# Filled waits, a gate spread by DMA and closer attention in a one-core attention and expert kernel

## The chip, the cores and the metric

The kernel runs on one core of a Trainium2 chip. A core has TensorE (PE) for matrix products into the accumulator memory (PSUM), VectorE (DVE), ScalarE (ACT) and GpSimd (POOL) for the rest, SyncE (SP) for issuing transfers, and 16 DMA engines. The metric is the device time of one execution in microseconds (us); before the change it is 210.46 us, the median of three runs (210.33 to 211.22).

## What is computed

Eight sequences of 576 positions and eight heads of 64 pass through a linear attention (softmax of q over the head's width, softmax of k over the positions), and then each whole sequence goes to one of eight experts, chosen from the mean of the attention's output:

```python
q_s = softmax(q, axis=-1)                       # [8, 8, 576, 64]
k_s = softmax(k, axis=2)
kv  = einsum('bhsd,bhse->bhde', k_s, v)
x   = einsum('bhsd,bhde->bhse', q_s, kv)        # then [8, 576, 512]
logits = x.mean(axis=1) @ w_gate                # [8, 8]
e = argmax(logits, axis=1); gate = softmax(logits)[e]
out[b] = gate[b] * (relu(x[b] @ w1[e[b]]) @ w2[e[b]])   # w1 [512, 1024], w2 [1024, 512]
```

For the inputs drawn here the experts are 2, 3, 3, 1, 3, 3, 4, 6, so five of the eight sequences need an expert that is not yet in the core's memory.

## The kernel before

A sequence has two units n = 2b and 2b + 1 of four heads each. For a unit q, k and v are loaded by SyncE (576 KB each), ScalarE takes the exponentials, VectorE sums q, GpSimd casts v and scales q, TensorE makes the products "kv" and the transposes of q, and then two products x. A gate follows the second unit: it picks the expert, and GpSimd issues the loads of w1 and w2, which are cast to 16 bits on the way. The expert of sequence b takes 17 steps; the work of later sequences is put between the steps by a table of ticks, where one expert spans 17 ticks. [...] The first two sequences' attention runs ahead of the table (the prologue). Cuts are marked; `in_pool` has three buffers each for q, k and v, the pool of output tiles has four, and the PSUM banks are: "mm" three, "kv" two, "ht" one, "x" one of double width.

```python
    def load(n, names="qkv"):
        if n >= 2 * B:
            return
        b, i = divmod(n, 2)
        for name in names:
            x = in_pool.tile([128, 2, J * Dh], FP32, name=f"{name}_in")
            nc.sync.dma_start(out=x, in_=pair_src({"q": q, "k": k, "v": v}[name], b, i))
            ins[n, name] = x.rearrange("p n (j d) -> p n j d", j=J)
    # ... cut ...
    def kv_mm(n):
        ek, va, kps = halves[n]["ek"], v_aug[n % NVB], kv_banks(n)
        for j in range(J):
            for g in range(2):
                r = slice(64 * g, 64 * g + 64)
                nc.tensor.matmul(
                    kps[g][:, 0:129], lhsT=ek[r, j], rhs=va[r, j],
                    start=(j == 0), stop=(j == J - 1),
                )
    # ... cut ...
    def t_mm(n):
        eq, kps = halves[n]["eq"], t_banks(n)
        for j in range(J):
            for g in range(2):
                r = slice(64 * g, 64 * g + 64)
                tp = kps[g].bitcast(FP16)[:, 448:448 + S]
                nc.tensor.transpose(out=tp[:, 64 * j:64 * j + 64], in_=eq[r, j], identity=ident[r, r])
    def t_out(n, g):
        tp = t_banks(n)[g].bitcast(FP16)[:, 448:448 + S]
        qt = qt_pool.tile([128, S], FP16, name="qt")
        if n < 4 or (n < 8 and g == 1):
            nc.scalar.copy(qt, tp)
        else:
            nc.vector.tensor_copy(out=qt, in_=tp)
        halves[n]["qt"][g] = qt
    # ... cut ...
    # x_step(n, g), sequence b = n // 2, c = 2 * (n % 2) + g
        kvs, qts = halves[n]["kv"], halves[n]["qt"]
        px = bank("x")
        nc.tensor.matmul(px[:, 0:SM], lhsT=kvs[g], rhs=qts[g][:, 0:SM], start=True, stop=True)
        nc.tensor.matmul(px[:, SM:S], lhsT=kvs[g], rhs=qts[g][:, SM:S], start=True, stop=True)
        if b < 2:
            if c == 0 or n == 3:
                nc.vector.tensor_copy(out=xt[:, c, :], in_=px[:, 0:S])
            else:
                nc.scalar.copy(xt[:, c, :], px[:, 0:S])
        else:
            nc.vector.tensor_tensor_reduce(
                out=xt[:, c, :], in0=px[:, 0:S], in1=ones_f32.to_broadcast([128, S]),
                scale=1.0, scalar=0.0, op0=ALU.mult, op1=ALU.add, accum_out=pooled[:, c:c + 1],
            )
    # ... cut ...
    # q_sum_step(n): sums of scaled q, a bank 'mm' and a bank 'ht' for a sequence
        qbar = seqs[b]["qbar"]
        for g in range(2):
            c = 2 * i + g
            r = slice(64 * g, 64 * g + 64)
            qb = seqs[b]["qb"][g][:, 4 * i:4 * i + 4]
            for j in range(J):
                nc.tensor.matmul(
                    qb, lhsT=eq[r, j], rhs=qhl[r, j].rearrange("p h n -> p (h n)"), start=(j == 0), stop=(j == J - 1)
                )
    # ... cut ...
    def gate_step(b):
        pooled = seqs[b]["pooled"]
        pg = kv_banks(2 * b + 1)[0][:, 136:144] if b > 1 else seqs[b]["qb"][0][:, 64:96]
        for c in range(ND):
            nc.tensor.matmul(
                pg[0:1, 0:E], lhsT=pooled[:, c:c + 1], rhs=wg_sb[:, c, :],
                start=(c == 0), stop=(c == ND - 1),
            )
        mx8 = gat_pool.tile([1, 8], FP32, name="mx8")
        nc.vector.max(out=mx8, in_=pg[0:1, 0:E])
        eidx = gat_pool.tile([1, 8], U32, name="eidx")
        nc.vector.max_index(out=eidx, in_max=mx8, in_values=pg[0:1, 0:E])
        # ... history of experts, slot, whether the expert is fresh (small VectorE steps) ...
        nc.vector.tensor_copy(out=hist[:, slot:slot + 1], in_=eidx[0:1, 0:1])
        zz = gat_pool.tile([1, E], FP32, name="zz")
        nc.vector.tensor_copy(out=zz, in_=pg[0:1, 0:E])
        # ... expert number into a GpSimd register, then two or four DMAs of w1 ...
    # ... cut ...
    def warm(count):
        pw = bank("ht")
        for n in range(count):
            nc.tensor.matmul(pw[:, 0:128], lhsT=ident, rhs=blkmask, start=True, stop=True)
    def hold_loads(b):
        nc.sync.dma_start(out=held, in_=w1_all[64:65, b, ND - 1, F - 8:F])
    def gate_exp(b):
        ex = gat_pool.tile([1, E], FP32, name="ex")
        sm = gat_pool.tile([1, 1], FP32, name="sm")
        nc.scalar.activation(out=ex, in_=seqs[b]["zz"], func=AF.Exp, bias=seqs[b]["nmx"], scale=1.0 / S, accum_out=sm)
        seqs[b]["sm"] = sm
    # ... cut ...
    def gate_spread(b):
        pb = bank("x")
        nc.tensor.matmul(pb[:, 0:2], lhsT=ones_row, rhs=seqs[b]["hl"], start=True, stop=True)
        gate = gat_pool.tile([128, 1], FP32, name="gate")
        nc.vector.tensor_single_scalar(out=gate, in_=pb[:, 1:2], scalar=1.0 / 2048.0, op=ALU.mult)
        nc.vector.tensor_tensor(out=gate, in0=gate, in1=pb[:, 0:1], op=ALU.add)
        seqs[b]["gate"] = gate
    # ... cut ...
    # fetch(b, w_all, part): VectorE copies the expert from the slot that holds it (onto itself if fresh)
    # moe(b): the expert on one sequence, 17 steps: 8 groups, 4 blocks in two halves, a tail
            phm = bank("mm")
            fsl = slice(fc * 128, (fc + 1) * 128)
            for c in range(ND):
                nc.tensor.matmul(
                    phm, lhsT=w1_sb[:, c, fsl], rhs=xt[:, c, 0:SM],
                    start=(c == 0), stop=(c == ND - 1),
                )
            for c in range(ND):
                nc.tensor.matmul(
                    pht[:, fc * ST:(fc + 1) * ST], lhsT=w1_sb[:, c, fsl], rhs=xt[:, c, SM:S],
                    start=(fc == 0 and c == 0), stop=(fc == NF - 1 and c == ND - 1),
                )
        ...
        gate = seqs[b]["gate"]
        for st in range(4):
            po = bank("mm")
            for fc in range(NF):
                nc.tensor.matmul(
                    po, lhsT=hsb[:, fc, st * 128:st * 128 + 128], rhs=w2_sb[:, fc, :],
                    start=(fc == 0), stop=(fc == NF - 1),
                )
                if fc == 3:
                    yield
            osb = o_pool.tile([128, D], FP32, name="osb")
            nc.scalar.mul(osb, po, gate)
            for jj in range(2):
                nc.sync.dma_start(out=out_p[b, :, 2 * st + jj], in_=osb[64 * jj:64 * jj + 64])
            yield
    # ... cut ...
    # the table: at(t, function, arguments)
    # at_gate(t, b): gate_step at t, gate_exp t + 3, gate_split t + 4, gate_spread t + 6
    at(0, pool_step, 1)
    at(1, t_step, 2)
    at_gate(0.2, 1)
    at(0.4, hold_loads, 1)
    at(0.4, load, 4)
    at(0.4, load, 5)
    at(0.4, load, 6)
    at(0.3, mul_q, 2, nc.vector)
    at(2.5, mul_q, 3, nc.vector)
    at(2, x_step, 2, 0)
    at(3, x_step, 2, 1)
    at(4.5, t_step, 3)
    at(6, x_step, 3, 0)
    at(7, x_step, 3, 1)
    at(13, load_w2, 1)
    at(5, gate_exp, 0)
    at(5.5, gate_split, 0)
    at(6.5, gate_spread, 0)
    places = [(19.5, 24), (29.5, 34), (39.5, 44.5), (56, 61), (73, 78), (90, 95)]
    for b in range(2, B):
        for i in range(2):
            n, t = 2 * b + i, places[b - 2][i]
            at(t, kvt_step, n)
            for g in range(2):
                at(t + 2 + 2 * g, x_step, n, g)
            at(t - 5.35, exp_q, n)
            at(t - (5.35 if n < 8 else 8), cast_v, n)
            at(t - 4.35, exp_k, n)
            if n + 3 < 2 * B:
                at(t - 4.35, load, n + 3)
            at(t - 4.7, scale_q, n, nc.gpsimd)
        at_gate(places[b - 2][1] + 5, b)
    # ... cut ...
    with tc.manual_schedule(engines={ET.PE, ET.DVE, ET.Activation, ET.Pool, ET.SP}):

        warm(55)
        # ... attention of the first two sequences, unit by unit ...
        q_sum_step(3)
        kv_step(3)
        for b in range(B):
            for m, _ in enumerate(moe(b)):
                run_ticks(NU * b + m + 1)
```

## Time and profile before

| | before |
|---|---|
| time, median of 3 | 210.46 us |
| span of the profiled execution | 209.2 us |
| first product of the first expert | 26.7 us |
| second expert's first product | 52.4 us |
| TensorE's last product | 204.1 us |
| bytes moved by DMA | 48.56 MB |

The page of a profile gives each engine's busy time and share of the span, then the span in 40 slices of 5.2 us, in which a digit is a busy share in tenths; PEclk is the clock granted to TensorE in tenths of full speed. Waits are listed as "engine line <- what released it: total us, times, longest". The chain of waits follows the work that ended last back through what released each piece. A line such as L435 is a line of the kernel's file: L181 is the products "kv", L202 the transposes, L241 the products x, L294 the gate's product, L401 the product that spreads the gate, L435 and L440 the expert's first layer, L454 and L469 its second, L418 the copy of an expert, L119 a load, L463 and L476 the stores, L380 the held load. SPq, POOLq and ACTq are the issuing queues. In the list of groups, the costliest on GpSimd, VectorE and ScalarE are these:

```profile
L444 ACT ACTIVATE hsb<-mm 128x512 f16<-128x512 f32 x64 | 37.5, 593 | 26.6 <-PE mm L435 26.0
L461 ACT ACTIVATE osb<-mm,gate 128x512 f32<-128x512 f32 x32 | 21.9, 687 | 40.1 <-PE mm L454 33.1
L154 POOL TENSOR_TENSOR eq<-eq,qsi 128x1152 f16<-128x1152 f16 x13 | 27.5, 2119 | 36.2 <-DVE qsi L143 19.8
...
L141 DVE TENSOR_REDUCE qs<-eq 128x18 f32<-128x1152 f16 x16 | 21.5, 1346 | 16.1 <-ACT eq L124 16.1
```

Behind the count stand the busy time in us and the mean of one in ns, then the idle time of the engine just before, and what ended most of it.

### The profile page before, as it was taken

The numbers are of one execution on the slowest core, as the hardware profiler recorded it, in microseconds if no ns is written. First come the engines' busy times: TensorE is split into PE (matmuls) and PEld (weight loads), VectorE is DVE, ScalarE is ACT, GpSimd is POOL, SyncE is SP. The second block draws the span as 40 slices with busy tenths as digits, with TensorE's granted clock in tenths as the row PEclk, the third lists the DMA queues.
The fourth block names the chain that finished last, engine by engine and source line by source line (L and its number), as shares of the span: only waits on it lengthen the run. The fifth ranks groups of instructions, "written<-read, shape, count | busy, mean of one in ns | idle before, by whom it ended". The sixth has DMA issues, their size and how long they took to land.

```text
span 209.2 us, 4699 instructions
## 1 busy us (share of the span) xinstructions
PE 176.8 (85%) x1743; PEld 96.1 (46%) x1743; DVE 112.7 (54%) x378; ACT 112.8 (54%) x178; POOL 62.2 (30%) x71
## 2 busy tenths in 40 slices
PE   6455798979979489488999679998999899999990
PEld 6443544434535146244455334564555455445440
DVE  0667853461484767538665476766669663222000
ACT  2686514836766535745349613892398146536630
POOL 2163905000760650232905151156047405000000
PEclk9955555999999969979999999999999999999998
DMA  6999999999989999776999994592469947996054
GB/s 181 380 391 392 130 183 191 182 231 387 395 318 301 403 393 382 265 238 140 185 293 273 372 395 106 115 326 64 98 106 188 214 119 136 194 190 200 0 128 99
DMA packets 28583, 48.56 MB, mean 232 GB/s; under 512 B 2960, under 2 KB 10128, under 8 KB 28560
## 3 DMA queue, kind: packets, MB, share of 16 engines
q1 hardware_dynamic: 19472, 37.76, 54.0%
q0 software_dynamic: 8544, 10.49, 31.8%
q8 instruction: 13, 0.21, 0.4%
q10 hardware_dynamic: 544, 0.02, 0.2%
q14 instruction: 10, 0.08, 0.1%
HBM read 61.88 MB, written 9.44 MB: 341 GB/s over the span
## 4 chain that ended last, share of the span: by engine, by line
PE 45%; DMA 25%; DVE 21%; issue 4%; ACT 2%; SPq 1%; POOL 0%; POOLq 0%; DVEq 0%; ACTq 0%
PE mm L454 17%; PE mm L435 14%; DMA w_all<-in_moe_w_dram 12%; DMA q_in<-in_q_dram 7%; DVE qs L141 6%; DMA v_in<-in_v_dram 6%; PE kv L181 4%; PE mm L469 3%; DVE w_all L418 2%; PE x L241 2%; DVE kv L191 2%; PE ht L440 2%; DVE qt L210 2%; ACT eq L124 2%; DVE qsi L143 1%
## 5 line engine op out<-in xcount | busy, mean ns | idle before, releaser
L435 PE MATMUL mm<-xt,w_all 128*128 128x512 f16 x256 | 69.2, 402 | 1.4 <-ACT hsb L444 1.4
L454 PE MATMUL mm<-w_all,hsb 128*128 128x512 f16 x256 | 61.9, 387 | 0.1
L444 ACT ACTIVATE hsb<-mm 128x512 f16<-128x512 f32 x64 | 37.5, 593 | 26.6 <-PE mm L435 26.0
L461 ACT ACTIVATE osb<-mm,gate 128x512 f32<-128x512 f32 x32 | 21.9, 687 | 40.1 <-PE mm L454 33.1
L154 POOL TENSOR_TENSOR eq<-eq,qsi 128x1152 f16<-128x1152 f16 x13 | 27.5, 2119 | 36.2 <-DVE qsi L143 19.8
L454 PEld LDWEIGHTS <-hsb 128*128 128x128 f16 x256 | 23.3, 99 | 27.3 <-issue 2.1
L435 PEld LDWEIGHTS <-w_all 128*128 128x128 f16 x256 | 21.2, 101 | 21.3 <-issue 6.0
L141 DVE TENSOR_REDUCE qs<-eq 128x18 f32<-128x1152 f16 x16 | 21.5, 1346 | 16.1 <-ACT eq L124 16.1
L418 DVE COPY w_all<-w_all 128x2048 f16 x28 | 21.6, 773 | 15.1 <-DMA w_all<-in_moe_w_dram 14.4
L132 POOL CAST va<-v_in 128x1152 f16<-128x1152 f32 x15 | 18.5, 1233 | 32.0 <-PE mm L469 17.4
L250 DVE CUSTOM_DVE_ANT_0 xt<-x,ones_f 128x576 f16<-128x576 f32 x24 | 17.8, 743 | 14.6 <-PE x L242 14.6
L440 PEld LDWEIGHTS <-w_all 128*128 128x128 f16 x256 | 17.0, 101 | 17.0 <-issue 3.3
L241 PE MATMUL x<-qt,kv 128*128 128x512 f16 x32 | 13.4, 419 | 10.2 <-DVE pooled L250 4.5
L346 POOL DMA_DIRECT2D w_all<-in_moe_w_dram x18 | 8.0, 448 | 46.0 <-DVE nmx L328 22.9
L124 ACT ACTIVATE eq<-q_in 128x1152 f16<-128x1152 f32 x16 | 18.5, 1159 | 2.1 <-DMA q_in<-in_q_dram 2.1
L136 ACT ACTIVATE ek<-k_in 128x1152 f16<-128x1152 f32 x16 | 18.6, 1164 | 0.5 <-DMA k_in<-in_k_dram 0.5
L440 PE MATMUL ht<-xt,w_all 128*128 128x64 f16 x256 | 18.6, 197 | 0.0
L181 PE MATMUL kv<-va,ek 64*128 64x129 f16 x288 | 13.8, 241 | 3.4 <-DVE zz L323 3.3
L208 ACT COPY qt<-kv 128x576 f16<-128x576 f16 x10 | 6.1, 638 | 14.6 <-DVE kv L191 11.6
L181 PEld LDWEIGHTS <-ek 64*128 64x128 f16 x288 | 10.2, 105 | 6.9 <-issue 6.2
L191 DVE SCALAR_TENSOR_TENSOR kv<-kv,icv,blkmask 128x128 f16<-128x128 f32 x32 | 11.2, 351 | 1.2
L189 DVE RECIPROCAL icv<-kv 128x1 f32<-128x1 f32 x32 | 5.1, 158 | 8.7 <-PE kv L202 7.2
(80 smaller groups left out, 141.0 us busy)
## 6 DMA issues: line engine op xcount, KB each, us to landing
w_all<-in_moe_w_dram POOLq DMA_DIRECT2D x30, 512.0 KB
q_in<-in_q_dram SPq DMA_DIRECT2D x16, 576.0 KB, 6.5
k_in<-in_k_dram SPq DMA_DIRECT2D x16, 576.0 KB, 7.6
v_in<-in_v_dram SPq DMA_DIRECT2D x16, 576.0 KB, 8.8
out_dram<-osb SPq DMA_DIRECT2D x64, 128.0 KB, 4.3
w_all<-in_moe_w_dram POOLq DMA_DIRECT2D x4, 256.0 KB
out_dram<-osb_t SPq DMA_DIRECT2D x16, 64.0 KB, 2.4
wg_sb<-in_moe_w_gate_dram ACTq DMA_DIRECT2D x2, 8.0 KB, 5.3
```

What stands on the lines that cost most here:

```text
L124: nc.scalar.activation(out=eq.rearrange("p j n d -> p n j d"), in_=ins.pop((n, "q")), func=AF.Exp)
L132: nc.gpsimd.tensor_copy(out=dst, in_=ins.pop((n, "v")))
L136: nc.scalar.activation(out=ek.rearrange("p j n d -> p n j d"), in_=ins.pop((n, "k")), func=AF.Exp)
L141: nc.vector.tensor_reduce(out=qs, in_=halves[n]["eq"], op=ALU.add, axis=AX.X)
L154: eng.tensor_tensor(out=eq, in0=eq, in1=qsi.unsqueeze(3).to_broadcast([128, J, 2, Dh]), op=ALU.mult,)
L181: nc.tensor.matmul(kps[g][:, 0:129], lhsT=ek[r, j], rhs=va[r, j], start=(j == 0), stop=(j == J - 1),)
L418: copy = nc.vector.tensor_copy(out=w_all[:, b % NS, cs, fs], in_=w_all[:, ds(seqs[b]["src"], 1), cs, fs].rearrange("p o c f -> p (o c) f"),)
L435: nc.tensor.matmul(phm, lhsT=w1_sb[:, c, fsl], rhs=xt[:, c, 0:SM], start=(c == 0), stop=(c == ND - 1),)
L440: nc.tensor.matmul(pht[:, fc * ST:(fc + 1) * ST], lhsT=w1_sb[:, c, fsl], rhs=xt[:, c, SM:S], start=(fc == 0 and c == 0), stop=(fc == NF - ...
L444: nc.scalar.activation(out=hsb[:, fc, 0:SM], in_=phm, func=AF.Relu)
L454: nc.tensor.matmul(po, lhsT=hsb[:, fc, st * 128:st * 128 + 128], rhs=w2_sb[:, fc, :], start=(fc == 0), stop=(fc == NF - 1),)
L461: nc.scalar.mul(osb, po, gate)
```

## The change

Four things change together. Idle products ("warm") are put ahead of products that wait in the prologue, with counts set by the table FILL, and the opening run grows from 55 to 80; their results are not used, they keep TensorE active. The gate's value is spread over the 128 partitions by a small DMA from ScalarE's queue, where before it went as two halves through a product and two VectorE steps; and the gate's product moves from a "kv" bank to the "x" bank, with its copy taken earlier. The attention of the third and fourth sequences (units 4 to 7) moves closer together in the table, with one of each unit's two x results taken out of PSUM by ScalarE and the transposed q all by VectorE. Loads from unit 7 on are issued later and further apart. The numbers of the units' ticks are in `places`.

```diff
@@ -108,6 +108,9 @@
 
     out_p = out.rearrange("b (p j) d -> b p j d", j=J)
 
+
+    FILL = {("qsum", 0): 0, ("t", 0): 24, ("qsum", 1): 18, ("x", 0, 0): 8, ("qsum", 2): 30, ("qsum", 3): 14}
+
     ins, halves, seqs, issued, copies = {}, {}, {}, {}, {}
 
     def load(n, names="qkv"):
@@ -195,6 +198,7 @@
 
     def t_mm(n):
         eq, kps = halves[n]["eq"], t_banks(n)
+        warm(FILL.get(("t", n), 0), kps[0][:, 144:208])
         for j in range(J):
             for g in range(2):
                 r = slice(64 * g, 64 * g + 64)
@@ -204,7 +208,7 @@
     def t_out(n, g):
         tp = t_banks(n)[g].bitcast(FP16)[:, 448:448 + S]
         qt = qt_pool.tile([128, S], FP16, name="qt")
-        if n < 4 or (n < 8 and g == 1):
+        if n < 4:
             nc.scalar.copy(qt, tp)
         else:
             nc.vector.tensor_copy(out=qt, in_=tp)
@@ -238,6 +242,7 @@
         xt, pooled = seqs[b]["xt"], seqs[b].get("pooled")
         kvs, qts = halves[n]["kv"], halves[n]["qt"]
         px = bank("x")
+        warm(FILL.get(("x", c, b), 0), px[:, 640:768])
         nc.tensor.matmul(px[:, 0:SM], lhsT=kvs[g], rhs=qts[g][:, 0:SM], start=True, stop=True)
         nc.tensor.matmul(px[:, SM:S], lhsT=kvs[g], rhs=qts[g][:, SM:S], start=True, stop=True)
         if b < 2:
@@ -246,6 +251,8 @@
                 nc.vector.tensor_copy(out=xt[:, c, :], in_=px[:, 0:S])
             else:
                 nc.scalar.copy(xt[:, c, :], px[:, 0:S])
+        elif n < 8 and g:
+            nc.scalar.activation(out=xt[:, c, :], in_=px[:, 0:S], func=AF.Copy, accum_out=pooled[:, c:c + 1])
         else:
             nc.vector.tensor_tensor_reduce(
                 out=xt[:, c, :], in0=px[:, 0:S], in1=ones_f32.to_broadcast([128, S]),
@@ -261,6 +268,7 @@
             seqs.setdefault(b, {})["qb"] = [bank("mm"), bank("ht")]
             seqs[b]["qbar"] = gat_pool.tile([128, ND, 2, 4], FP16, name="qbar")
         qbar = seqs[b]["qbar"]
+        warm(FILL["qsum", n], seqs[b]["qb"][1][:, 256:384])
         for g in range(2):
             c = 2 * i + g
             r = slice(64 * g, 64 * g + 64)
@@ -288,8 +296,7 @@
 
     def gate_step(b):
         pooled = seqs[b]["pooled"]
-
-        pg = kv_banks(2 * b + 1)[0][:, 136:144] if b > 1 else seqs[b]["qb"][0][:, 64:96]
+        pg = bank("x") if b > 1 else seqs[b]["qb"][0][:, 64:96]
         for c in range(ND):
             nc.tensor.matmul(
                 pg[0:1, 0:E], lhsT=pooled[:, c:c + 1], rhs=wg_sb[:, c, :],
@@ -300,6 +307,8 @@
         nc.vector.max(out=mx8, in_=pg[0:1, 0:E])
         eidx = gat_pool.tile([1, 8], U32, name="eidx")
         nc.vector.max_index(out=eidx, in_max=mx8, in_values=pg[0:1, 0:E])
+        zz = gat_pool.tile([1, E], FP32, name="zz")
+        nc.vector.tensor_copy(out=zz, in_=pg[0:1, 0:E])
         slot = b % NS
         sidx = None
         if b:
@@ -319,8 +328,6 @@
             sidx = gat_pool.tile([1, 8], U32, name="sidx")
             nc.vector.max_index(out=sidx, in_max=top, in_values=score)
         nc.vector.tensor_copy(out=hist[:, slot:slot + 1], in_=eidx[0:1, 0:1])
-        zz = gat_pool.tile([1, E], FP32, name="zz")
-        nc.vector.tensor_copy(out=zz, in_=pg[0:1, 0:E])
 
         gone = (b + 2) % NS
         nc.vector.memset(hist[:, gone:gone + 1], -1.0)
@@ -369,11 +376,13 @@
             )
         part_loads(b)
 
-    def warm(count):
-
-        pw = bank("ht")
+    def warm(count, pw=None):
+
+        if pw is None:
+            pw = bank("ht")[:, 0:128]
+        width = pw.shape[1]
         for n in range(count):
-            nc.tensor.matmul(pw[:, 0:128], lhsT=ident, rhs=blkmask, start=True, stop=True)
+            nc.tensor.matmul(pw, lhsT=ident, rhs=blkmask[:, 0:width], start=True, stop=True)
 
     def hold_loads(b):
 
@@ -385,23 +394,15 @@
         nc.scalar.activation(out=ex, in_=seqs[b]["zz"], func=AF.Exp, bias=seqs[b]["nmx"], scale=1.0 / S, accum_out=sm)
         seqs[b]["sm"] = sm
 
-    def gate_split(b):
+    def gate_value(b):
         gt = gat_pool.tile([1, 1], FP32, name="gt")
         nc.vector.reciprocal(out=gt, in_=seqs[b]["sm"])
-        hl = gat_pool.tile([1, 2], FP16, name="hl")
-        nc.vector.tensor_copy(out=hl[:, 0:1], in_=gt)
-        nc.vector.tensor_scalar(
-            out=hl[:, 1:2], in0=hl[:, 0:1], scalar1=gt, scalar2=-2048.0, op0=ALU.subtract, op1=ALU.mult
-        )
-        seqs[b]["hl"] = hl
+        seqs[b]["gt"] = gt
 
     def gate_spread(b):
 
-        pb = bank("x")
-        nc.tensor.matmul(pb[:, 0:2], lhsT=ones_row, rhs=seqs[b]["hl"], start=True, stop=True)
         gate = gat_pool.tile([128, 1], FP32, name="gate")
-        nc.vector.tensor_single_scalar(out=gate, in_=pb[:, 1:2], scalar=1.0 / 2048.0, op=ALU.mult)
-        nc.vector.tensor_tensor(out=gate, in0=gate, in1=pb[:, 0:1], op=ALU.add)
+        nc.scalar.dma_start(out=gate, in_=seqs[b]["gt"].to_broadcast([1, 128]))
         seqs[b]["gate"] = gate
 
     def fetch(b, w_all, part):
@@ -491,8 +492,8 @@
     def at_gate(t, b):
         at(t, gate_step, b)
         at(t + 3, gate_exp, b)
-        at(t + 4, gate_split, b)
-        at(t + 6, gate_spread, b)
+        at(t + 4.5, gate_value, b)
+        at(t + 6.5, gate_spread, b)
 
     at(0, pool_step, 1)
     at(1, t_step, 2)
@@ -509,23 +510,23 @@
     at(6, x_step, 3, 0)
     at(7, x_step, 3, 1)
     at(13, load_w2, 1)
-    at(5, gate_exp, 0)
-    at(5.5, gate_split, 0)
-    at(6.5, gate_spread, 0)
-    places = [(19.5, 24), (29.5, 34), (39.5, 44.5), (56, 61), (73, 78), (90, 95)]
+    at(1.5, gate_exp, 0)
+    at(2.7, gate_value, 0)
+    at(4.7, gate_spread, 0)
+    places = [(20, 23.5), (27, 31), (40, 45), (56, 61), (73, 78), (90, 95)]
     for b in range(2, B):
         for i in range(2):
             n, t = 2 * b + i, places[b - 2][i]
             at(t, kvt_step, n)
             for g in range(2):
-                at(t + 2 + 2 * g, x_step, n, g)
+                at(t + 2 + g * (1.5 if n < 8 else 2), x_step, n, g)
             at(t - 5.35, exp_q, n)
             at(t - (5.35 if n < 8 else 8), cast_v, n)
             at(t - 4.35, exp_k, n)
-            if n + 3 < 2 * B:
-                at(t - 4.35, load, n + 3)
             at(t - 4.7, scale_q, n, nc.gpsimd)
-        at_gate(places[b - 2][1] + 5, b)
+            if n >= 7:
+                at(max(places[(n - 3) // 2 - 2][(n - 3) % 2] - 4.3, t - 15), load, n)
+        at_gate(places[b - 2][1] + (4.7 if b < 4 else 5), b)
         at(places[b - 2][1] + 9, load_w2, b)
     for b in range(1, B):
         for part in range(2):
@@ -549,7 +550,7 @@
     load(2)
     with tc.manual_schedule(engines={ET.PE, ET.DVE, ET.Activation, ET.Pool, ET.SP}):
 
-        warm(55)
+        warm(80)
         exp_q(0)
         sum_q(0)
         q_sum_step(0)

```

## The prediction

> **What bounds the kernel now.** I read the page first (busy shares, the row of slices), then TensorE's waits, then the chain of waits in order of time, then the timelines of TensorE and of the load queue, and asked in each stage which wait ends last.
>
> The page:
>
> ```profile
> PE 176.8 (85%) x1743; PEld 96.1 (46%) x1743; DVE 112.7 (54%) x378; ACT 112.8 (54%) x178; POOL 62.2 (30%) x71
> ...
> PEclk9955555999999969979999999999999999999998
> DMA  6999999999989999776999994592469947996054
> ```
>
> TensorE is the busiest engine, but 32 us of the 209.2 us span it is idle, and in slices 3 to 7 (about 10 to 37 us) it runs at half clock. The DMA engines are busy almost without a break in the first 125 us. So there are two bounds: transfers in the first half, TensorE in the second.
>
> TensorE's waits by stage, 0 to 70, 70 to 130 and 130 to 210 us:
>
> ```profile
> PE mm L269 <- DVE qhl L149: 4.9, 4, 2.3
> PE kv L202 <- DVE eq L154: 2.7, 2, 1.8
> PE mm L435 <- ACT hsb L444: 1.4, 1, 1.4
> ```
>
> ```profile
> PE kv L181 <- DVE zz L323: 3.3, 2, 1.9
> PE x L241 <- DVE pooled L250: 3.0, 2, 1.8
> PE x L241 <- DVE gate L404: 3.0, 1, 3.0
> PE x L241 <- DVE qt L210: 1.7, 1, 1.7
> ```
>
> ```profile
> PE x L241 <- DVE pooled L250: 1.5, 2, 0.9
> ```
>
> The columns are the total in us, times, and the longest. The 11.0 us of the middle stage are the target: 3.3 because a gate shares the "kv" bank with the next sequence's products, 3.0 because the gate's spreading matmul takes TensorE and the "x" bank. From 131.7 us on only 1.5 us are lost.
>
> The chain, in order of time (start, us):
>
> ```profile
> 32.82 9.04 DMA w_all<-in_moe_w_dram
> ...
> 42.76 6.56 DMA q_in<-in_q_dram
> 49.38 12.39 DMA v_in<-in_v_dram
> ...
> 102.35 15.40 DMA w_all<-in_moe_w_dram
> ```
>
> The third sequence's loads (units 4 and 5) may start only when the second sequence's first weights have landed (41.9 us, the held load), and then queue: unit 4's q lands at 49.3, its v at about 52.4, unit 5's v at 56.9, unit 6's v at 61.8 us. The last line is the fourth sequence's w2: issued from 101.6, landed at 117.85 us, and the in-order VectorE stood before it from 113.2 us.
>
> TensorE's timeline where the third and fourth sequences enter:
>
> ```profile
> 55.45 0.70 PE L181 MATMUL kv<-va,ek 64*128 64x129 f16 x18
> 55.99 0.43 PE L202 MATMUL kv<-ident,eq 64*128 64x64 f16 x18
> ...
> 63.68 0.70 PE L181 MATMUL kv<-va,ek 64*128 64x129 f16 x18
> ```
>
> ```profile
> 73.83 0.69 PE L181 MATMUL kv<-va,ek 64*128 64x129 f16 x17 [1.89 <-DVE zz L323]
> ...
> 81.67 0.70 PE L181 MATMUL kv<-va,ek 64*128 64x129 f16 x18
> ```
>
> These are units 4, 5, 6, 7. Units 4 and 5 come 3 and 7 us after their last input; unit 6 comes 12 us after its v, by its place in the program, not by a transfer.
>
> **What the skill says.** The Trainium skill, "TensorE: Matmul & The Clock Gate", Part 1, says the clock is halved by default, full after some 3.4 us of sustained activity and halved again after an idle window of that length. The trace agrees on the way up: after 33.2 us, with no gap, the clock was full at about 37.2. On the way down it is stricter: waits of 1.0 and 1.8 us (7.3 to 8.3 and 8.9 to 10.7) were enough, the clock was 0.50 from 10 us. So I count gaps of about 3 us, or two near each other, as a fall. The same page's Part 4 says that transposes don't count as activity in the same way; nothing here separates that. "DMA: Bandwidth & Descriptors", Anatomy of one DMA, gives a fixed cost of about 2 us; the smallest output stores here take 2.4 us at the median. It thus costs more latency than the matmul it replaces, but on no compute engine. Its specifications put the memory limit per core at about 358 GB/s; the trace moves 380 to 403 GB/s, and the trace decides.
>
> **The change part by part.**
>
> (1) Fill. The 55 warm-up matmuls took 5.41 us, 98 ns on average. The same page's Part 1 gives 107 ns for this width cold and 56 ns warm, which fits a mix; as an estimate, 25 more at 56 ns end at 7.30 + 1.4 = 8.7 us, 0.4 us after their successor is ready (8.26). The 24, 18, 8, 30 and 14 fills take by the same figure at most 1.3, 1.0, 0.45, 1.7 and 0.8 us, in waits of 1.83, 1.32, 0.73, 2.32 and 0.26 us; only the last overruns, by up to 0.5 us. If the clock stays full, the first four groups of the first expert cost 1.0 instead of 2.0 us, about 4 us, with transposes and x products 4.5. They cannot start earlier, since the first weights land at 26.7 us. Against this, the transposes of unit 2 wait longer for VectorE's multiply (about 2.0 instead of 0.84 us).
>
> (2) Spreading the gate by DMA removes the two waits of 1.03 and 0.44 us at 42 us. By (1) and (2) the first expert ends at about 47.1 instead of 52.4 us: 26.75 + 8 groups of 0.98 + transposes and x products 1.6 + gate 0.4 + waits 2.6 = 39.2, then 6.9 and 1.0 us.
>
> (3) Most of that is given back at unit 4. Its values land at 52.4 us whatever TensorE does; GpSimd needs 1.16 us for the cast and 2.12 us for the multiply, so its transposes start at 55.7 us, as before (55.99). TensorE arrives there at about 51 us with four groups done instead of three, so 1.0 us is kept, and the wait can cost up to 2 us of cold clock. I count 0 for parts (1) to (3) together.
>
> (4) Closer attention. From 56.3 us on: unit 5 needs v at 56.9 + 1.16 + 2.12 = 60.2 and runs at 60.7 to 61.7 (before to 64.6, one group further): gain 1.9 us. Unit 6 is ready at 61.8 + 1.16 + 2.12 = 65.1, and TensorE is there at 65.8. Unit 7's loads now stand behind all ten stores of the first sequence; I expect q at 67 and v at 70, ready at about 71.7, TensorE there at 71.0. The second expert ends at about 74 us; VectorE has some 19 us of work in these 18 us, so I add 2 us: 76 instead of 80.75 us, with unit 7 already done, which before came after. Gain so far 4.75 + 1.4 (one unit: 0.64 + 0.31 + two x of 0.22).
>
> (5) The third expert with units 8 and 9: 15.9 + 2 x 1.4 + gate 0.3 + 1.0 = 20 us, so the fourth starts at 96 instead of 108.7 us. What goes is the 2.98 and 1.39 us of waits and their cold clock (88.3 to 92 us, 1.5 us), with unit 7's work.
>
> (6) The fourth expert's weights. Its gate comes after the second group of the third expert, at about 78.5 us instead of 94.7. Weights then fly from 80 us; they share with units 10 and 11 and the stores, 22 us before, so w2 lands at about 101, needed by VectorE at 100 and TensorE at 104. So the stall at 118 to 123 us (1.75 + 1.23) goes: 20 us for the fourth expert with units 10 and 11, and the fifth starts at 116 instead of 131.7 us.
>
> (7) From there the order is nearly unchanged: 77.5 us, less some tenths for the spreading matmul. Sum: 116 + 77.5 = 193.5 us of span; the measured time was 1.26 us above the span (210.46 to 209.2), so 194.8, and 195 with a little for the cold wait of (3).
>
> **Rivals.** (a) Transfers become the bound throughout. By the fourth expert's second half they must have carried 12 units (21.2 MB), three experts (12.6 MB as read; 4.2 each, since weights are read as 32 bits) and three sequences' stores (3.5 MB): 37.3 MB at 390 GB/s is 96 us, with the start and the gap at 20 to 22 us about 101, against my 104. There is little slack; if queue order wastes 5 us, the time is 199 to 201. The load queue speaks for it: its stores waited 5.5 us on v loads. (b) VectorE, 19 us of work in 18 us of the dense stage, or ScalarE held by its own small DMA issues, becomes the bound: 2 to 4 us more, 197 to 199. (c) The fills delay real work and the early wait at unit 4 keeps the clock low: nothing is gained before 60 us and 2 us are lost, 197. (d) Nothing is gained, since the same stalls return elsewhere: 208 to 211. Against it speaks that 6.3 us of the middle waits come from banks that are no longer shared in that way.
>
> **Range and chances.** All rivals but (d) stay under 203 us. If the dense stage fits without the 2 us of (4) and the cold clock does not return, 191. I say 195 us, 190 to 203 in 8 of 10. Faster by over 2% needs under 206.3: 0.93; within 2%: 0.05; slower: 0.02.
>
> **What would show it.** A clock of 1.0 from 10 to 40 us and the first expert's second half from about 39 us show (1) and (2). A wait of TensorE of 3 to 5 us ahead of unit 4's products, which stay at 54 to 57 us, shows (3); if they come before 53, (3) is wrong and the time lower. Units 6 and 7 at about 66 and 71.5 us show (4). Weights of the fourth expert in flight at 80 to 101 us, and no VectorE wait for them, show (6); a wait there is rival (a). The waits on the gate's spread and on its copy from the "kv" bank should be gone.

## The result and the profile after

The changed kernel takes 201.04 us, the median of four runs (200.41 to 202.59); four runs of the kernel before on the same chip took 210.41 us (210.33 to 211.22). The ratio is 0.956, with a 95% interval of 0.950 to 0.962. That is 9.4 us gained, of 15.5 that the prediction promised. The profiled run is the slowest of the four (202.59 us, a span of 200.9), so its moments lie up to 2 us later than those of a typical run. Its mean granted clock is also the lowest, 0.964 against 0.978 to 0.979 in the other three. The reader should keep that in mind wherever a single moment is read.

The page of the changed kernel: busy times, and two rows of the span in 40 slices of 5.0 us.

```profile
PE 176.4 (88%) x1854; PEld 98.1 (49%) x1854; DVE 114.0 (57%) x342; ACT 112.8 (56%) x182; POOL 61.9 (31%) x71
...
PEclk9999965899999969999999999999999999999999
DMA  5999999999996997988999959794999966995054
```

TensorE does the same work (176.4 us) in a span that is 8.3 us shorter. The clock row, half speed in slices 3 to 7 before, is full up to 25 us; then it falls after all, in slices 6 and 7 (25 to 35 us), just when the first expert begins, and once more in slice 15 (70 to 75 us). In the other three executions, whose mean clock is higher, the loss was probably smaller; they have no trace.

TensorE's waits of the changed kernel, at 0 to 70 us and at 70 to 125 us (total in us, times, longest):

```profile
PE mm L277 <- DVE qhl L152: 2.5, 3, 1.2
...
PE x L246 <- DVE pooled L257: 1.8, 1, 1.8
PE kv L206 <- DVE eq L157: 1.8, 2, 1.0
```

```profile
PE x L301 <- ACT xt L255: 3.0, 1, 3.0
PE x L246 <- DVE pooled L257: 1.9, 2, 1.6
```

The two causes that the change aimed at are gone: no wait on the gate's spread, none on its copy out of the "kv" bank. In their place stands a new one of 3.0 us, the gate's product (L301), which now takes an "x" bank and gets it only when ScalarE has taken the last x product out. TensorE's timeline shows where:

```profile
54.12 0.70 PE L184 MATMUL kv<-va,ek 64*128 64x129 f16 x18
...
60.21 0.38 PE L246 MATMUL x<-qt,kv 128*128 128x512 f16 x1 [1.84 <-DVE pooled L257]
60.55 0.70 PE L184 MATMUL kv<-va,ek 64*128 64x129 f16 x18
...
65.61 0.70 PE L184 MATMUL kv<-va,ek 64*128 64x129 f16 x18
70.51 0.35 PE L301 MATMUL x<-wg_sb,pooled 128*1 128x8 f32 x8 [2.96 <-ACT xt L255]
...
76.09 0.38 PE L246 MATMUL x<-qt,kv 128*128 128x512 f16 x1 [1.62 <-DVE pooled L257]
77.29 0.70 PE L184 MATMUL kv<-va,ek 64*128 64x129 f16 x18
```

The four "kv" lines are units 4, 5, 6 and 7. Units 4, 5 and 6 come as predicted (54 to 57, 60.7, 65.8 us); unit 7, predicted at 71.5, comes at 77.3. What follows inherits that:

| start of (us) | before | predicted | after |
|---|---|---|---|
| second expert | 52.4 | 47.1 | 50.1 |
| third expert | 80.6 | 76 | 80.7 (unit 7 already done) |
| fourth expert | 108.7 | 96 | 102.0 |
| fifth expert | 131.6 | 116 | 123.4 |
| from there to the end of the span | 77.6 | 77.5 | 77.5 |

The starts are those of the expert's first product in TensorE's timeline; the prediction's 80.75 and 131.7 were up to 0.2 us later.

Why unit 7 came late is read from three views of this run. First ScalarE's timeline:

```profile
67.03 1.16 ACT L127 ACTIVATE eq<-q_in 128x1152 f16<-128x1152 f32 x1 [3.43 <-DMA q_in<-in_q_dram]
68.10 0.67 ACT L462 ACTIVATE osb<-mm,gate 128x512 f32<-128x512 f32 x1
68.67 1.15 ACT L139 ACTIVATE ek<-k_in 128x1152 f16<-128x1152 f32 x1
69.72 0.64 ACT L255 ACTIVATE xt<-x 128x576 f16<-128x576 f32 x1
```

ScalarE stood 3.43 us before unit 7's q, and then did three things before the copy that frees the bank (the last line). The copy's input, an x product, had been ready at 65.7 us. Second, the load queue:

```profile
48.58 0.72 SPq L122 DMA_DIRECT2D v_in<-in_v_dram  x1
49.62 11.90 SPq L464 DMA_DIRECT2D out_dram<-osb  x8
61.61 1.19 SPq L477 DMA_DIRECT2D out_dram<-osb_t  x2
62.85 0.58 SPq L122 DMA_DIRECT2D q_in<-in_q_dram  x1
```

Unit 7's q is issued at 62.85 us, behind ten stores of the first expert that took 13 us to issue. For 7.5 us of these the queue waited for earlier loads (v, k and q, in waits of 3.3, 2.2 and 2.0 us), for 0.8 us for ScalarE. Before the change this q was issued at 62.30 us, so the load hardly moved; the change moved the unit's place towards it. Third, the chain of waits, which branches off at ScalarE; the second column is the length of the piece:

```profile
48.58 12.45 DMA v_in<-in_v_dram
...
62.85 4.10 DMA q_in<-in_q_dram
67.03 1.17 ACT eq L127
68.23 1.36 DVE qs L144
...
72.68 2.06 DVE score L321
...
75.29 0.73 DVE xt L257
76.09 0.38 PE x L246
...
93.34 16.35 DMA w_all<-in_moe_w_dram
```

The chain runs from q through VectorE, not through ScalarE's copy. VectorE stood 3.63 us before the sums of q (68.23 us) and came to the gate's steps only at 71.46 us, after the gate's product (70.51 to 70.86 us); so TensorE's wait of 3.0 us for ScalarE is not what ended last. One gate step, L321, works on eight numbers and took 2 us. It held the copy of the next x product (L257) until 75.29 us, and for that copy TensorE waited the 1.62 us at 76.09. So the late q held both ScalarE and VectorE. The last line, the fourth expert's w2 in flight from 93.3 to 109.7 us, matters below.

### The profile page after: what moved, and what is told of

The parts are those of the page before. It is cut to its first block, busy times and chain, and to the rows that moved or that the text cites. A ratio compares the mean times of both kernels' runs of the same rounds, so it can differ in the third digit from the quotient of the medians.

```text
span 200.9 us, 4888 instructions
## 1 busy us (share of the span) xinstructions
PE 176.4 (88%) x1854; PEld 98.1 (49%) x1854; DVE 114.0 (57%) x342; ACT 112.8 (56%) x182; POOL 61.9 (31%) x71
## 4 chain that ended last, share of the span: by engine, by line
PE 42%; DMA 21%; DVE 21%; issue 6%; ACT 4%; POOL 2%; SPq 1%; POOLq 1%; ACTq 0%; DVEq 0%
PE mm L455 18%; PE mm L436 14%; DMA w_all<-in_moe_w_dram 11%; DMA v_in<-in_v_dram 6%; DVE qs L144 5%; DMA q_in<-in_q_dram 4%; DVE w_all L419 4%; PE mm L470 2%; PE x L246 2%; ACT eq L127 2%; DVE qt L214 2%; PE ht L441 2%; DVE xt L257 2%; PE kv L184 2%; DVE same L316 1%
## 5 line engine op out<-in xcount | busy, mean ns | idle before, releaser
L436 PE MATMUL mm<-xt,w_all 128*128 128x512 f16 x256 | 66.9, 393 | 0.7 <-DMA w_all<-in_moe_w_dram 0.6
L419 DVE COPY w_all<-w_all 128x2048 f16 x28 | 25.7, 918 | 18.0 <-DMA w_all<-in_moe_w_dram 15.7
L135 POOL CAST va<-v_in 128x1152 f16<-128x1152 f32 x15 | 17.6, 1174 | 44.9 <-DMA v_in<-in_v_dram 28.7
L436 PEld LDWEIGHTS <-w_all 128*128 128x128 f16 x256 | 21.0, 100 | 19.8 <-issue 4.0
L441 PEld LDWEIGHTS <-w_all 128*128 128x128 f16 x256 | 16.7, 100 | 16.0 <-issue 1.6
L257 DVE CUSTOM_DVE_ANT_0 xt<-x,ones_f 128x576 f16<-128x576 f32 x20 | 14.8, 741 | 7.0 <-PE x L247 7.0
L246 PE MATMUL x<-qt,kv 128*128 128x512 f16 x32 | 12.7, 395 | 6.4 <-DVE pooled L257 5.6
L385 PEld LDWEIGHTS <-ident 128*128 128x128 f16 x174 | 11.0, 109 | 2.2 <-POOL ident masks.py:199 1.6
L385 PE MATMUL ht<-blkmask,ident 128*128 128x128 f16 x142 | 10.4, 243 | 1.9 <-POOL blkmask L73 1.9
L184 PE MATMUL kv<-va,ek 64*128 64x129 f16 x288 | 11.6, 219 | 0.2 <-DVE kv L194 0.2
L214 DVE COPY qt<-kv 128x576 f16<-128x576 f16 x24 | 10.7, 447 | 0.0
```

The lines of the kernel that those rows point to most:

```text
L257: nc.vector.tensor_tensor_reduce(out=xt[:, c, :], in0=px[:, 0:S], in1=ones_f32.to_broadcast([128, S]), scale=1.0, scalar=0.0, op0=ALU.mult ...
L385: nc.tensor.matmul(pw, lhsT=ident, rhs=blkmask[:, 0:width], start=True, stop=True)
L419: copy = nc.vector.tensor_copy(out=w_all[:, b % NS, cs, fs], in_=w_all[:, ds(seqs[b]["src"], 1), cs, fs].rearrange("p o c f -> p (o c) f"),)
L436: nc.tensor.matmul(phm, lhsT=w1_sb[:, c, fsl], rhs=xt[:, c, 0:SM], start=(c == 0), stop=(c == ND - 1),)
L441: nc.tensor.matmul(pht[:, fc * ST:(fc + 1) * ST], lhsT=w1_sb[:, c, fsl], rhs=xt[:, c, SM:S], start=(fc == 0 and c == 0), stop=(fc == NF - ...
```

## The experiments

All times are medians of four to six runs, each with the kernel before in the same batch on the same chip. Its median was 210.4 beside the changed kernel, and 210.7, 211.0 and 211.6 us in the three batches, so the ratios are what is compared between batches. One hundredth of the ratio is 2.1 us. Executions in which the chip was disturbed are left out. The ratios are those of means, and in e1 to e12 they leave out the profiled execution; the changed kernel's 0.956 has it in, and would be 0.955 without it. The changed kernel was run in the first batch only, so its comparison with e1 to e12 goes over the kernel before.

| | what differs | us | ratio (95% interval) |
|---|---|---|---|
| after | | 201.04 | 0.956 (0.950 to 0.962) |
| e1 | after, no fills | 202.40 | 0.963 (0.957 to 0.970) |
| e2 | after, gate spread by TensorE | 206.20 | 0.976 (0.971 to 0.981) |
| e3 | after, attention at its old places | 202.04 | 0.960 (0.955 to 0.965) |
| e4 | after, loads as before | 205.15 | 0.970 (0.964 to 0.976) |
| e5 | after, loads of unit 7 early | 199.43 | 0.949 (0.941 to 0.956) |
| e6 | after, x products taken out by VectorE | 200.32 | 0.952 (0.946 to 0.958) |
| e7 | e5 and e6 together | 199.52 | 0.946 (0.939 to 0.954) |
| e8 | before, with the gate's part alone | 206.64 | 0.980 (0.973 to 0.987) |
| e9 | after, 18 more fills in one wait | 200.21 | 0.947 (0.942 to 0.951) |
| e10 | e7 and e9 together | 201.59 | 0.950 (0.944 to 0.956) |
| e11 | before, with the spaced loads alone | 209.18 | 0.988 (0.983 to 0.993) |
| e12 | before, with gate and spaced loads | 203.56 | 0.962 (0.958 to 0.967) |

### Each part undone (e1 to e4)

**e1, no fills.**

```diff
-    FILL = {("qsum", 0): 0, ("t", 0): 24, ("qsum", 1): 18, ("x", 0, 0): 8, ("qsum", 2): 30, ("qsum", 3): 14}
+    FILL = {("qsum", n): 0 for n in range(4)}
-        warm(80)
+        warm(55)
```

> The changed kernel without its fills and with 55 opening products again. Theory W (the missing 6 us come from a new wait in the dense stage, 66 to 80 us, and the fills bring nothing that lasts): the first expert still starts at 26.7 us, held by its weights, unit 4's products stay near 54 us, held by v, and the time is 200 to 202 us, within 1% of the changed kernel's 201.0. Rival P (the fills bring most of the gain, and what is missing is the clock that fell at 26 us): without them the time is 204 us or more.

Without the fills the clock is low from about 10 to 35 us (0.63 at 10 to 15 us, 0.50 at 15 to 25, 0.67 at 25 to 35), and the first expert starts no later: its first product comes at 26.47 instead of 26.74 us, and the second expert at 49.4 instead of 50.1 us. The loss is 0.8 hundredths, 1.6 us, with intervals that overlap. The fills are worth little, and the sign is likely but not shown. The median lies 0.4 us above theory W's range and 1.6 us below that of theory P.

**e2, the gate spread by the matmul again.**

```diff
-        nc.scalar.dma_start(out=gate, in_=seqs[b]["gt"].to_broadcast([1, 128]))
+        pb = bank("x")
+        nc.tensor.matmul(pb[:, 0:2], lhsT=ones_row, rhs=seqs[b]["hl"], start=True, stop=True)
+        nc.vector.tensor_single_scalar(out=gate, in_=pb[:, 1:2], scalar=1.0 / 2048.0, op=ALU.mult)
+        nc.vector.tensor_tensor(out=gate, in0=gate, in1=pb[:, 0:1], op=ALU.add)
```

(and the split into two halves that feeds it; the gate's product stays in the "x" bank, so this undoes only the spread)

> The changed kernel with the gate spread by the matmul and two VectorE steps again; the gate's own product stays in the x bank. Theory W: the wait for the fifth line of unit 7's q is untouched, and the spread's own waits of before (1.0, 0.4 and 3.0 us) come back only in part, since the last of them was in a stage that is no longer ordered so: 201 to 204 us. Rival G (the DMA's latency and its wait on ScalarE cost more than the matmul did: 1.9 us at 43 us and 3.2 us at 109 us): the time falls below 200 us.

It costs 2.0 hundredths, 4.2 us, more than either text expected, and refutes rival G. TensorE's waits of this run at 70 to 125 us:

```profile
PE x L410 <- DVE pooled L257: 2.4, 1, 2.4
...
PE x L246 <- DVE gate L413: 2.1, 1, 2.1
```

L410 is the spreading matmul. At one sequence's spread (94.5 us) it has to wait for an "x" bank itself, 2.4 us; at another's (116.6 us) the next x product has to wait 2.1 us until VectorE has read the spread gate. So a spread by matmul can cost TensorE a wait ahead of it or behind it.

**e3, attention at its old places.** The old places of units 4 to 9, the old distance between x products, and the old split of the copies between VectorE and ScalarE.

```diff
-    places = [(20, 23.5), (27, 31), (40, 45), (56, 61), (73, 78), (90, 95)]
+    places = [(19.5, 24), (29.5, 34), (39.5, 44.5), (56, 61), (73, 78), (90, 95)]
-        if n < 4:
+        if n < 4 or (n < 8 and g == 1):
             nc.scalar.copy(qt, tp)
```

> The changed kernel with the old ticks of the third and fourth sequences' attention and the old split of its copies between VectorE and ScalarE; fills, spread by DMA, gate in the x bank and spaced loads stay. Theory W: the placing carries the gain of the stage 80 to 123 us (the fourth gate comes earlier and unit 7 is done before the third expert), so the time rises to 205 us or more, although the 3.0 us wait at 70 us goes. Rival B (the gain comes from the banks and the spread alone): 201 us or less.

This is my largest miss: undoing it costs 0.4 hundredths, within the noise. I had expected at least 205 us, and the rival at most 201; 202.04 is neither. The waits only move: 1.8 us at 66.4 and 1.7 us at 72.5 us instead of one of 3.0 at 70.5, and unit 7 comes at 76.4 instead of 77.3 us. Here unit 7 stands in the program behind the third expert's first group (75.4 us), and ScalarE takes its q at 66.16 us without a wait; this run also kept the full clock at 26 us, so its moments can't be compared one for one. Why the old places cost so little is not shown.

**e4, loads as before.** Each unit's loads are issued again three units ahead, not spaced.

```diff
-            if n >= 7:
-                at(max(places[(n - 3) // 2 - 2][(n - 3) % 2] - 4.3, t - 15), load, n)
+            if n + 3 < 2 * B:
+                at(t - 4.35, load, n + 3)
```

> The changed kernel with the old rule for loads (unit n + 3 is loaded 4.35 ticks before unit n). Theory W: load 7 is again ahead of the first sequence's last two stores, q of unit 7 lands some 0.5 us earlier, and later units' loads crowd the stores: within 1.5 us of 201.0. Rival L (spacing the loads carries the gain): 204 us or more.

It costs 1.4 hundredths, 3.0 us; my theory said within 1.5 us, and the median lies in the rival's range. VectorE's and TensorE's timelines in this run, where the fourth expert's w1 is cast:

```profile
102.74 1.42 DVE L419 COPY w_all<-w_all 128x2048 f16 x2 [3.74 <-DMA w_all<-in_moe_w_dram]
```

```profile
104.89 0.34 PE L301 MATMUL x<-wg_sb,pooled 128*1 128x8 f32 x8 [3.73 <-DVE pooled L257]
```

In both kernels GpSimd issues these weights at about 90 us (89.52 here, 90.14 in the changed kernel). In the changed kernel nothing is loaded by SyncE between 84.5 and 97.8 us, and the same cast runs at 99.54 us without a wait. Here six loads of 576 KB are issued in that stretch, at 86.5 to 88.1 and at 90.6 to 92.6 us, and the weights arrive at least 3 us later. VectorE stands before them, the x product behind them isn't taken out, and the gate's product waits 3.7 us.

### The late q of unit 7 (e5 to e7)

**e5, loads of unit 7 right behind those of unit 6**, ahead of the ten stores.

```diff
     at(0.4, load, 6)
+    at(0.4, load, 7)
-            if n >= 7:
+            if n >= 8:
```

> The changed kernel with unit 7 loaded right behind unit 6, ahead of the first sequence's stores. Theory Q (unit 7 is late because its loads stand behind ten stores that themselves wait for loads 4 to 6; q landing at 67.0 us holds ScalarE, and with it the evacuation that the third gate waits for): q of unit 7 lands near 63 us, v near 66 us, the 3.0 us wait of the gate's product at 70 us shrinks below 1 us, unit 7's products come at about 71 instead of 77.3 us, and the time is 195 to 198 us. Rival D (VectorE, GpSimd and the shared expert copies bound the dense stage anyway): less than 2 us is gained, 199 to 201.

ScalarE in this run, for comparison with the four lines shown of the changed kernel:

```profile
64.32 1.17 ACT L127 ACTIVATE eq<-q_in 128x1152 f16<-128x1152 f32 x1
65.54 0.69 ACT L462 ACTIVATE osb<-mm,gate 128x512 f32<-128x512 f32 x1
66.12 1.15 ACT L139 ACTIVATE ek<-k_in 128x1152 f16<-128x1152 f32 x1
67.17 0.64 ACT L255 ACTIVATE xt<-x 128x576 f16<-128x576 f32 x1
```

There is no wait for q any more. The gate's product comes at 68.4 us without a wait, unit 7 at 72.6 (predicted for the change itself: 71.5), the third expert at 76.7 (76) and the fourth at 98.0 (96). The order of work that the prediction had drawn up is there once q is in time. This profiled run also kept the clock at 26 us, but that doesn't explain it: at unit 6 it is 0.9 us behind the changed kernel's run (66.54 and 65.61 us), and the 4.0 us are gained between there and the third expert. In it GpSimd's multiply (67.41 to 69.53 us) is over before the gate's steps, and L321 takes 0.15 us.

But the ratio falls by only 0.7 hundredths (1.5 us), with overlapping intervals. That is what rival D had forecast; theory Q's 195 to 198 us did not come. So the late loads of unit 7 are shown as the cause of its late start, while their worth is only bounded: 0 to 4 us. The diff moves q, k and v together, so q and v aren't told apart.

**e6, x products of units 4 to 7 taken out by VectorE alone**, as before the change.

```diff
-        elif n < 8 and g:
-            nc.scalar.activation(out=xt[:, c, :], in_=px[:, 0:S], func=AF.Copy, accum_out=pooled[:, c:c + 1])
```

> The changed kernel with all x results of units 4 to 7 taken out by VectorE, as before; everything else stays. Theory Q: the gate's product no longer waits for ScalarE, so its wait at 70 us (3.0 us) goes, but VectorE, which waits for the same q, has four more steps of 0.74 us: 199.5 to 202 us. Rival S (moving the evacuation to ScalarE is what costs the 6 us): 198 us or less.

The gate's product still waits 2.2 us at 70.2 us, now for VectorE, which stood 2.6 us before unit 7's q sums (67.78 us) and took the product out only behind them (69.41). That is what the theory of the late q said. Giving ScalarE half of these copies was neither the cause nor a gain that can be measured.

**e7, both.** The two diffs above together.

> Both edits of the two runs before: unit 7 loaded behind unit 6, and all x results of units 4 to 7 by VectorE. Theory Q: with q there early, ScalarE is no longer held and the move to VectorE brings nothing more: within 1.5 us of the run with unit 7 early alone. Rival S: at least 2 us below it.

199.52 us and the lowest ratio, but not distinguishable from e5. Its profiled run had the low clock at 26 us (second expert at 49.5 us) and shows the same as e5: unit 7 at 72.7 us, the third expert at 76.1. A new wait of 2.1 us on the gate's product at 98.6 us takes back part of the gain: the fifth expert starts at 121.2, against 119.1 us in e5.

### The parts by themselves, and the clock at 26 us (e8 to e12)

**e8, the gate's part alone** in the kernel before: spread by the small transfer, the product in the "x" bank, and its steps at the new times.

```diff
-        pg = kv_banks(2 * b + 1)[0][:, 136:144] if b > 1 else seqs[b]["qb"][0][:, 64:96]
+        pg = bank("x") if b > 1 else seqs[b]["qb"][0][:, 64:96]
-        (spreading matmul and its two VectorE steps)
+        nc.scalar.dma_start(out=gate, in_=seqs[b]["gt"].to_broadcast([1, 128]))
```

> The kernel before with the gate part alone: spread by DMA, gate's product in the x bank, copy of the logits taken early; no fills, old placing, old loads. If the parts add up, as the runs that undo one each say (the spread's return cost 5 us, the loads' return 4 us, the placing's return 1 us, the fills' return 1 us), this gives 205 to 207 us. If the gate part carries all of it: 202 us or less. If it pays only together with the spaced loads: 208 us or more.

206.64 us, 2.0 hundredths below the kernel before. Both waits that the change aimed at are gone in its trace (3.3 us for the gate's copy, 3.0 us for its spread). It is the same 4.2 us that undoing the spread cost in e2, though e8 moves the gate's product out of the "kv" bank as well; what that move brings alone was not run.

**e9, 18 more fills** in the last wait of the prologue.

```diff
-    FILL = {..., ("qsum", 2): 30, ("qsum", 3): 14}
+    FILL = {..., ("qsum", 2): 30, ("qsum", 3): 32}
```

> After the change, with 32 instead of 14 idle matmuls ahead of the last query sums of the prologue (18 more, at 61 ns each 1.1 us, in a wait that was 1.23 us and behind which the clock fell at 26 us). Everything else is as in the changed kernel. Theory W (idle matmuls are worth little): the clock stays at 1.0 from 10 to 40 us, the first expert's first four groups take 1.0 instead of 1.87 us and it ends at about 47 instead of 50.1 us, but the fourth unit counted from zero is then held by its values and GpSimd's multiply until about 53, so of 3 us at most 1 to 1.5 stay by then, and the time is 200 to 201 us. Rival F (the clock's fall is what the prediction missed): the 3 us come through to the end, 197.5 to 198.5 us.

Stretches of the changed kernel and of e9 at 26 to 38 us (busy us of PE, PEld, DVE, ACT, POOL; then the granted clock, the share of the DMA engines, GB/s):

```profile
26.00:38.00 12.00, 10.21 (x77) 4.76 (x71) 5.94 (x23) 4.24 (x9) 2.73 (x4) 0.57 1.13 181
```

```profile
26.00:38.00 12.00, 9.83 (x128) 5.65 (x123) 6.51 (x28) 6.87 (x16) 2.73 (x4) 1.00 1.17 196
```

In the changed kernel a wait of 1.23 us was left at 23.3 us, behind the 14 fills, and a further 0.16 and 0.56 us before the first weights; from 26 us the clock was half. In e9 the clock stays full, and TensorE's timeline shows the first expert as the prediction had drawn it (second half from 39.2, second expert at 47.1 us):

```profile
39.18 7.07 PE L455 MATMUL mm<-w_all,hsb 128*128 128x512 f16 x32
...
47.18 1.04 PE L436 MATMUL mm<-xt,w_all 128*128 128x512 f16 x4
...
52.97 0.70 PE L184 MATMUL kv<-va,ek 64*128 64x129 f16 x18
```

And then it is given back: of 2.9 us at the second expert 1.15 are left at unit 4 (52.97 instead of 54.12). What holds it is ScalarE's timeline, in order before unit 4's q:

```profile
47.71 1.16 ACT L127 ACTIVATE eq<-q_in 128x1152 f16<-128x1152 f32 x1 [2.46 <-DMA q_in<-in_q_dram]
48.78 0.67 ACT L462 ACTIVATE osb<-mm,gate 128x512 f32<-128x512 f32 x1
```

Further on it is 0.8 us at the third expert (79.85), 0.9 at the fourth (101.13) and 1.2 at the fifth (122.20). That is what theory W said of the give-back. The time of 200.2 us lies in its range (200 to 201), but this batch was slower; by the ratio it is 199.1 on the scale of the first, between W and rival F (197.5 to 198.5). The interval of the ratio overlaps that of the changed kernel by 0.001: a gain of about 2 us is likely, not shown.

This one trace doesn't show the 18 fills at work, because the wait that they fill was short in it anyway (section on the prediction, (1)). What speaks for them is the mean clock of the other five executions: 0.985 to 0.990, where the changed kernel had 0.978 to 0.979.

**e10, e7 and e9 together.**

> All three amendments together: loads of unit 7 right behind those of unit 6, x products of units 4 to 7 taken out by VectorE alone, and 32 instead of 14 idle matmuls ahead of the last query sums of the prologue. The first two together took 199.5 us. Theory W: the fill adds at most 1 us, 198.5 to 199.5 us. Rival F: 196.5 to 197.5 us, with the first expert ending at about 47 and the third starting at about 74.5 us.

201.59 us, higher than either of its parts and outside both expectations; its interval overlaps those of both, and that of the changed kernel. In its profiled run the opening came late: the 80 warm-up matmuls took 7.26 us (6.42 in the changed kernel's run), the transposes behind them waited 1.9 us for VectorE (1.0 there), and the second sequence's gate product came 1.3 us later than in e9 (29.5 against 28.2 us). Why the opening varies so between executions was not settled. The three amendments don't add up within what can be measured.

**e11, the spaced loads alone**, and **e12, gate and spaced loads** without fills and without the closer attention.

> The kernel before, with nothing but the spaced loads (units 8 to 11 loaded two units later than before; unit 7 at the place of the fourth unit or 15 units of time ahead of its own). Undoing the spaced loads in the changed kernel cost 4.4 us. If the parts add up (theory A), this takes 206 to 207 us. If the spacing pays only because the other parts bring the fourth expert's weights forward into the same stretch as units 10 and 11 (rival I, interaction), it brings less than 1.5 us: 209 to 211 us, since in the kernel before the fourth expert's weights came at 94 to 118 us anyway.

> The changed kernel without the fills (none, and 55 warm-up matmuls) and without the closer attention (old places, old split of the copies): so the gate's part and the spaced loads alone. Theory: these two carry the result; undoing fills cost 1.4 us and undoing the placing 1.0 us, so 202 to 204 us, of the 9.4 us gained 7 to 8. Rival: fills and placing only look small one at a time, since each makes up for the other; then without both it is 205 us or more.

e11 gains 1.2 hundredths (2.6 us) and falls between my two theories as written. Against what undoing the loads cost by the ratios, 1.4 hundredths, it is the same; the 4.4 us in the expectation was a difference of medians from different batches. So the parts add up within the intervals, and an interaction isn't needed. e12 settles the sum: gate and loads bring 3.8 hundredths of the 4.4, 8.0 us of 9.3, while e8 and e11 one by one bring 2.0 and 1.2. In e12 the clock is at half speed from 10 to 35 us as in the kernel before, and units 4 to 9 stand at their old places.

## Why the prediction came out as it did

The direction and the order of magnitude came from the right place. The two bank waits of the middle stage (6.3 us) were the target; the gate's part removes them (e8), and its spread alone costs 4.2 us when it is undone (e2). 201 us lies inside 190 to 203; but 195 was 6 us too low, and part of the reasoning gave the credit to the wrong piece. In the profiled run the fifth expert starts 7.4 us later than predicted: 4.7 us are there at the third expert, and the third and fourth experts take 21.3 and 21.4 us instead of 20. What makes these two longer was not traced.

**(1) Fills.** The steps up to 22 us hold, with one term mis-sized: I took the last wait from the kernel before, 0.26 us, and expected its fill to overrun. It was 0.94 us of fill and 1.23 us of idle time. TensorE, now at full clock, came to this wait 2.0 us earlier than before and VectorE 1.1 us earlier, which is what the fill covers. The idle time is nearly all of one VectorE step, which TensorE waits for:

```profile
23.37 1.13 DVE L152 TENSOR_TENSOR qhl<-qsi,qhl 128x18 f16<-128x18 f32 x1
23.32 1.16 POOL L135 CAST va<-v_in 128x1152 f16<-128x1152 f32 x1 [0.87 <-DMA v_in<-in_v_dram]
```

The step ends 0.02 us after GpSimd's cast. In e5, e9 and e10 the cast was over when the step began; there it took 0.18 us, and in e5, with the same 14 fills, the wait was 0.28 us. So without the meeting of the two, by this estimate, the 0.26 us would have been about right. In the changed kernel's run the clock fell at 26 us, behind this gap; the first expert's first groups cost 1.87 us after all, and it ended at 50.1 instead of 47.1 us. e9, whose clock stayed full, has the second expert at 47.18 us.

**(2), (3) Given back at unit 4.** Right in the main, and the most useful step of the prediction: it kept me from crediting 5 us to the fills. In e9 the 2.9 us shrink to 1.15 at unit 4, by a wait for unit 4's transfers; I had counted 0. The sign that I named for it didn't appear in the changed kernel: TensorE came to unit 4 so late (54.1 us) that no wait of 3 to 5 us was left ahead of it. And where the opening was quicker, unit 4 came before 53 us (52.97 in e9, 52.66 in e5, 50.92 in e3), which I had called a sign against (3).

**(4) Closer attention.** The step that failed, in size and in cause: the third expert starts at 80.7 instead of 76 us. I put q of unit 7 at 67 us, which is exact (ScalarE took it at 67.03), and v at 70 (GpSimd took it at 71.48), but made unit 7 ready at 71.7. By the 1.16 and 2.12 us that I had used for units 5 and 6 it is 73.3 from my own date of v, and 74.7 from the measured one. I also didn't see that ScalarE and VectorE would stand before that q with the older sequence's work behind it: ScalarE 3.43 us, with the copy that frees the bank for the gate's product, and VectorE 3.63 us, with the gate's steps and the next x copy. One of these steps then ran beside unit 7's GpSimd multiply and took 2.04 instead of 0.15 us. As a rough sum, 3.0 and 1.6 us of waits and some 1.5 us of low clock (3.5 us busy at 0.57 in 70 to 74 us), less the 2 us that I had allowed for VectorE, make 4.1 of the 4.7 us by which the third expert misses 76, though the 3.0 us, as the chain shows, aren't what ended last. e5 and e7 bring unit 7's loads earlier and get 76.7 and 76.1. And the closer places bring no gain that can be measured: undoing them costs 0.8 us, within the noise (e3). The 2 us that I added for a crowded VectorE were of another kind, described in the last section.

**(5), (6) The fourth expert.** Its weights fly at 90 to 110 us, not at 80 to 101. A gate's product at 83.45 (predicted 78.5) explains 5 of the 10 us. The rest is the way from the product to the issue: 6.7 us (83.45 to 90.14), where the kernel before took 2.75 (93.08 to 95.83) and I had put 1.5. VectorE was busy with unit 8's q sums until 85.75, for which it had stood 2.3 us, and then one step of the gate took 1.98 us. VectorE did wait for w2, which I had taken for a sign of rival (a): 3.5 us, until 109.78. But TensorE lost only 0.3, 0.2 and 0.7 us by it. Rival (a), transfers, is still the nearest of the four: the 201.04 us are at the upper end of its 199 to 201, the flight of w2 is on the chain, and e4 shows how close the margin is, as 3 us hang on when six loads are issued. I had hardly credited the spaced loads at all; they carry between a quarter and a third of the gain (1.2 to 1.4 of 4.4 hundredths).

**(7) The last 77.5 us.** Right: 77.5 us in the profiled run.

The Trainium skill, "DMA: Bandwidth & Descriptors", Anatomy of one DMA, gave me about 2 us of fixed cost. The section states it for transfers that GpSimd issues; the gate's are issued by ScalarE. The page of the changed kernel has the eight transfers at 6.2 us to landing (median; the columns are the operation, count, size, time to landing):

```profile
gate<-gt ACTq DMA_DIRECT2D x8, 0.5 KB, 6.2
```

The shortest took 2.8 us, the longest 7.3. At 44.8 us ScalarE waited 1.9 us for the first sequence's gate. None of TensorE's waits shown above is for it.

## What to carry to other kernels

When a wait is removed, ask what each engine stands in front of at that moment, and what stands behind it: here one late load held ScalarE and VectorE, behind them stood a copy and a gate's steps, and one of those steps took 2.04 us instead of 0.15 because of when it came. Where several parts of a change are on offer, take account of what they do in the stage that binds. The one that takes an operation off the critical engine (2.0 hundredths) and the one that keeps a critical transfer alone in its stretch (1.2 to 1.4) brought nearly everything here; filling waits in a stage that waits for data next, and moving work closer to inputs that are late, brought nothing clear of noise. Undo the parts one by one before giving any of them the credit.

## What the hardware showed that I had not expected

**Tiny VectorE steps that take 2 us.** VectorE in the changed kernel, and GpSimd beside it:

```profile
71.81 0.13 DVE L311 COPY zz<-x 1x8 f32<-1x8 f32 x1
71.92 0.73 DVE L316 SCALAR_TENSOR_TENSOR same<-hist,eidx 1x8 f32<-1x8 f32 x1
72.68 2.04 DVE L321 SCALAR_TENSOR_TENSOR score<-same,own 1x8 f32<-1x8 f32 x1
```

```profile
71.48 1.16 POOL L135 CAST va<-v_in 128x1152 f16<-128x1152 f32 x1 [6.87 <-DMA v_in<-in_v_dram]
72.59 2.12 POOL L157 TENSOR_TENSOR eq<-eq,qsi 128x1152 f16<-128x1152 f16 x1
```

Both slow steps work on eight numbers and end within 0.02 us of the GpSimd operation that was running when they began: 72.65 against 72.64, and 72.68 + 2.04 = 72.59 + 2.12 + 0.01. Another gate's step L316, at 86.44, takes 1.98 us and ends with GpSimd's multiply of 86.29 to 88.41; alone these steps take 0.15 us (88.46). The copy L311 at 71.81, whose input is in PSUM, ran beside the same cast and took 0.13 us. The weight copy L419 at 57.02 us takes 2.46 instead of 0.69 us, beside a multiply that ends at 58.94. The Trainium skill has this: "SBUF — State Buffer", section "Who interferes with whom", says that a VectorE instruction with two inputs in that memory, or a copy in a mode that uses two ports, contends with a GpSimd instruction that reads it; for the copy the one that starts second is blocked for the whole of the other. For the three small steps, and for the 128x18 step under (1), the trace agrees to 0.03 us; the copy, begun 0.2 us after the multiply, ends 0.54 us after it, and so seems to have done little before. My surcharge of 2 us for a busy VectorE should have been this: as an estimate from the 2.04 and 1.98 us, a gate one of whose steps meets a GpSimd multiply loses about 2 us between the product and the weights' issue. It is a matter of timing: in e5 and e7 the third gate's steps met none.

**The clock can be lost to a gap of about 1 us.** The wait ahead of the last query sums of the prologue (1.23 us in the changed kernel, with 0.2 and 0.6 us soon after) was between 0.91 and 1.23 us in the profiled runs of after, e2, e4, e6 and e7, and in these the clock fell at 26 us. In e3 (0.70 us), e5 (0.28), e9 and e10 it stayed full. These are single runs that differ in other things too, and no threshold is established by them; the Trainium skill, "TensorE: Matmul & The Clock Gate", Part 1, names an idle window of about 3.4 us, and here less was enough.
